# A fused convolution and token-mixing kernel: the transposes of u in the full final steps moved from TensorE to crossbar DMA transfers, and the channel mixes placed later

## The chip, the cores and the metric

The kernel runs on one NeuronCore of a Trainium2 chip. The rounds of runs fell on several chips; every ratio compares runs of the same rounds. Times are device microseconds of that core. Where a median is quoted, the number of runs stands beside it.

## The reference, cut to what matters

```python
# x: [8, 4224, 192] f32, a 7-tap softmax-weighted causal convolution comes first
x = lightweight_conv(x, weight)
theta = x @ w_theta
zr, zi = x * cos(theta), x * sin(theta)
y = einsum('ts,bsd->btd', w_tok_r, zr) + einsum('ts,bsd->btd', w_tok_i, zi)   # 4224 x 4224 each
u = x + y
out = u + maximum(u @ w_ch, 0)          # the channel mix
```

The last line is what the change is about. `u @ w_ch` contracts over the channels, and the kernel's matmul for it takes u with its channels on the partitions; the token mixing leaves u with tokens on the partitions. Every piece of u has to be transposed between the two.

## The kernel before

The token mixing runs in 58 steps. A step takes two blocks of 128 output rows and up to 11 chunks of 128 input tokens. A step with two blocks makes seven runs over the chunks (a seven-product scheme: two 2x2 block products in seven), each run two matmuls a chunk, y. (In this sense a run is a part of a step; elsewhere a run is an execution of a kernel.) After a run DVE adds the PSUM result into `pv` ("give"). DVE also prepares the weights of the next step: it turns four weight blocks (`turn`, a transpose on DVE) and makes four sums or differences of turned blocks (`wsum`, S1 to S4). The steps 41 to 57 are "final": they complete their rows, and the step after them casts u to f16 on ACT, transposes it on TensorE, copies it out of PSUM on ACT, mixes the channels (matmuls v) and stores. The steps 41 to 52 have all 11 chunks ("full final steps"); 53 to 57 have fewer and are called late.

```python
    def transposed(u, by_dve=False):
        tp = banks("tp", F16)
        for k in range(6):
            pe(nc.tensor.transpose(
                tp[:, 0, k * P : (k + 1) * P], u[:, k * P : (k + 1) * P], ident
            ))
        uT = wk.tile([P, 6, P], F16, name="uT", tag="uT")          # 2 buffers
        evacuate(uT[:, :, :].rearrange("p k s -> p (k s)"), tp[:, 0, 0 : 6 * P], by_dve)
        return uT
# [cut]
        def w_tasks(self):          # the weight blocks of the NEXT step, on DVE; time in units of runs
            return [
                (0.25, lambda: self.turn("11")), (1.2, lambda: self.turn("21")),
                (2.05, lambda: self.wsum("S3")), (2.2, lambda: self.turn("22")),
                (3.05, lambda: self.wsum("S1")), (3.3, lambda: self.wsum("S2")),
                (4.2, lambda: self.turn("12")), (5.1, lambda: self.wsum("S4")),
            ]
# [cut]
        def runs(self):             # weights, z, PSUM tile, opens it?, (row block, half, ...) of the sum
                return [
                    ("11", Z11, "c1", True, (0, 0, True)),
                    ("S1", T1, "c2", True, (1, 1, True)),
                    ("S2", T2, "c1", False, (0, 1, True)),
                    ("S4", Z22, "c2", False, (0, 1, False)),
                    ("S3", T3, "c1", False, (1, 1, False)),
                    ("12", Z21, "c3", True, (0, 0, False)),
                    ("22", T4, "c1", False, (1, 0, True)),
                ]
# [cut]
        def turn_u(self, i, g):
            self.uT[i, g] = transposed(self.ub[i, g])
# [cut]
        def outputs(self):
                # late steps: [cut]
                    at = 0.7 + 12 * i                      # us after the step's end, row block i
                    every, turn, mix = 3.6, 2.9, 4.7       # per column half g: cast, transpose, mix
                for g in range(NG):
                    found.append((at, lambda i=i, g=g: self.cast(i, g)))
                    found.append((at + turn, lambda i=i, g=g: self.turn_u(i, g)))
                    found.append((at + mix, lambda i=i, g=g: self.output(i, g)))
                    at += every
```

The PSUM tile c1 holds run 11, is then added to by run S2 (third) and by run S3 (fifth), and the sums are taken in between. So PE may not start run S3 before DVE has read c1 after run S2; this sum is called the third run's sum below. x is added to rows in two ways: for the steps 43 to 52 POOL adds a loaded tile (`xr`) to `pv` in SBUF, 3.1 us each, one step ahead, so during the steps 42 to 51; for the late steps an accumulating DMA, issued by POOL, adds x to the partial sums in DRAM, four steps ahead, so beside the steps 49 to 53. (For the steps 41 and 42 such transfers run ten steps ahead.)

## Time and profile before

| | before |
|---|---|
| median of 3 runs | 1468.77 us (1468.66 to 1469.96) |
| PE busy in the profiled run | 1434.6 us of 1469.8 |
| y matmul, start to start, in the final steps | 163 ns |
| v matmul, start to start | 82 ns |
| transpose, start to start | 56 ns |
| a full final step (steps 42 to 51) | 29.0 us |

The last four rows were worked out from the PE records of the trace: the median distance between starts, and the distance between the first y matmul of a step and that of the next. There are 7656 y matmuls in every kernel of this study, so steps can be laid side by side by counting them.

The page of the kernel before, its busy times and the chain that ended last:

```profile
PE 1434.6 (98%) x10095; PEld 905.6 (62%) x10095; DVE 1001.0 (68%) x1050; ACT 360.7 (25%) x461; POOL 430.3 (29%) x659
...
PE 91%; DVE 3%; ACT 3%; DMA 1%; issue 1%; POOL 0%; DVEq 0%; ACTq 0%; POOLq 0%
```

The table by stretches of the kernel before, for the steps 45, 51 and 52 (first column: from and to in us; the numbers follow the head line):

```profile
core 0: us, PE busy (x) PEld busy (x) DVE busy (x) ACT busy (x) POOL busy (x), PEclk, DMA share, GB/s
1137.40:1166.50 29.10, 29.10 (x213) 19.09 (x211) 22.20 (x19) 6.28 (x8) 10.83 (x10) 1.00 0.77 186
1311.90:1340.90 29.00, 29.00 (x212) 19.04 (x211) 25.61 (x19) 5.78 (x8) 15.53 (x16) 1.00 1.06 246
1340.90:1369.90 29.00, 29.00 (x212) 19.05 (x211) 18.25 (x19) 6.78 (x9) 8.19 (x12) 1.00 0.93 210
```

PE has no gap at all in these three steps: what is taken off it there should shorten the span. The DMA share is 0.77 in a middle step and about 1 in the last ones (it adds up packet times, so the 1.06 of step 51 means that packets of one engine overlapped).

Yet the trace held a warning: in step 48, where the sum ended at +16.62 us of the step in place of +16.09, PE did wait for it, 0.22 us just before run S3 (and in step 41 0.19 us). The author's list of waits from 1100 to 1380 us ends with step 48's:

```profile
PE y L408 <- DVE pv L373: 0.2, 1, 0.2
```

These are the 0.22 us that the prediction's 324.78 of 325 us lack.

### The profile page before, as it was taken

What the parts mean: (1) busy time and instruction counts of PE and PEld (TensorE: products, weight loads), DVE (VectorE), ACT (ScalarE), POOL (GpSimd) and SP (SyncE); (2) the same over time, 40 slices, a digit from 0 to 9 for tenths busy, and PEclk for the clock granted to TensorE, in tenths of its full rate; (3) what the DMA queues carried; (4) which work ended last, traced back from release to release, by engine and by line L of the source; (5) the groups of instructions that cost most, each with busy time, mean ns of one, the idle gap of its engine ahead of it and who ended that gap; (6) DMA issues with size and microseconds to landing.
All of it is one profiled execution on the core that took longest, in us unless ns stands there. A gap on an engine that the chain in (4) does not pass through costs nothing.

```text
span 1469.8 us, 24434 instructions
## 1 busy us (share of the span) xinstructions
PE 1434.6 (98%) x10095; PEld 905.6 (62%) x10095; DVE 1001.0 (68%) x1050; ACT 360.7 (25%) x461; POOL 430.3 (29%) x659
## 2 busy tenths in 40 slices
PE   7789999999999999999999999999999999999997
PEld 4556666666666666666666666666666666666665
DVE  6884655454548687766656658769777787778575
ACT  6861101111134353000000015254122222121224
POOL 7422211111223322211113232332233333453220
PEclk9999999999999999999999999999999999999998
DMA  9976756574699999887879989999778777999873
GB/s 172 227 155 145 144 104 144 96 151 89 149 232 212 232 224 263 193 198 167 209 162 239 200 194 229 201 232 256 128 191 197 173 182 185 224 237 217 196 201 108
DMA packets 234975, 274.16 MB, mean 187 GB/s; under 512 B 69104, under 2 KB 202608, under 8 KB 234864
## 3 DMA queue, kind: packets, MB, share of 16 engines
q0 software_dynamic: 163616, 95.30, 49.0%
q1 hardware_dynamic: 71248, 177.30, 34.1%
q8 instruction: 79, 1.29, 0.3%
q14 instruction: 32, 0.26, 0.1%
HBM read 245.49 MB, written 111.28 MB: 243 GB/s over the span
## 4 chain that ended last, share of the span: by engine, by line
PE 91%; DVE 3%; ACT 3%; DMA 1%; issue 1%; POOL 0%; DVEq 0%; ACTq 0%; POOLq 0%
PE y L408 81%; PE v L138 6%; PE tp L153 3%; ACT z L233 2%; PE pc L196 2%; DMA st<-in_moe_w_tok_i_dram 1%; DVE pv L373 1%; DVE z L244 1%; DVE z L238 0%; DVE wt L308 0%; DVE pv L437 0%; ACT uT L148 0%; DVE wt L320 0%; ACT pv L371 0%; ACT z L148 0%
## 5 line engine op out<-in xcount | busy, mean ns | idle before, releaser
L408 PE MATMUL y<-z,wt 128*128 128x384 f16 x7656 | 1295.3, 326 | 7.7 <-DVE pv L373 6.8
L408 PEld LDWEIGHTS <-wt 128*128 128x128 f16 x7656 | 737.5, 98 | 475.0 <-issue 10.4
L373 DVE TENSOR_TENSOR pv<-y,pv 128x768 f32<-128x768 f32 x324 | 308.5, 953 | 374.2 <-PE y L408 348.6
L308 DVE STREAM_TRANSPOSE wt<-st 128x1408 f16<-128x1408 f16 (+7 forms) x224 | 326.4, 1463 | 7.7 <-DMA st<-in_moe_w_tok_i_dram 7.0
L295 POOL DMA_DIRECT2D st<-in_moe_w_tok_i_dram x232 | 132.7, 581 | 497.7 <-DVE wt L308 473.7
L295 POOL DMA_DIRECT2D st<-in_moe_w_tok_r_dram x232 | 132.7, 581 | 459.0 <-DVE wt L308 443.7
L320 DVE TENSOR_TENSOR wt<-wt 128x1408 f16<-128x1408 f16 (+7 forms) x216 | 204.1, 945 | 9.5 <-PE y L408 6.6
L148 ACT ACTIVATE uT<-tp 128x768 f16<-128x768 f16 x127 | 102.3, 813 | 296.8 <-PE tp L153 294.9
L148 ACT ACTIVATE z<-pc 128x768 f16<-128x768 f32 x65 | 52.9, 814 | 386.5 <-PE pc L196 386.5
L371 ACT ACTIVATE pv<-y 128x768 f32<-128x768 f32 x66 | 53.7, 813 | 281.5 <-PE y L408 281.5
L138 PEld LDWEIGHTS <-uT 128*128 128x128 f16 x1056 | 93.0, 99 | 25.9 <-issue 9.9
L437 DVE SCALAR_TENSOR_TENSOR pv<-v,pv 128x768 f32<-128x768 f32 x66 | 62.7, 949 | 46.8 <-PE v L138 45.5
L183 POOL DMA_DIRECT2D xw<-in_x_dram x132 | 76.5, 591 | 35.8 <-issue 10.1
L427 ACT ACTIVATE ub<-pv 128x768 f16<-128x768 f32 x66 | 54.8, 837 | 90.6 <-DVE pv L373 89.5
L244 DVE TENSOR_TENSOR z<-z 128x768 f16<-128x768 f16 x132 | 73.4, 556 | 3.8
L233 ACT ACTIVATE z<-v,half_pi 128x768 f16<-128x768 f32 x66 | 59.6, 903 | 40.0 <-PE v L138 39.8
L238 DVE TENSOR_TENSOR z<-z 128x1536 f16<-128x1536 f16 x66 | 60.4, 950 | 10.8 <-ACT z L233 10.8
L355 POOL TENSOR_TENSOR pv<-pv,xr 128x1536 f32<-128x1536 f32 x20 | 62.9, 3144 | 7.9 <-issue 4.5
L138 PE MATMUL v<-wch,uT 128*128 128x192 f16 x528 | 56.9, 254 | 3.5 <-DVE pv L437 1.9
L138 PE MATMUL v<-wth,uT 128*128 128x192 f16 x528 | 54.3, 246 | 3.1 <-ACT z L233 3.0
L233 ACT ACTIVATE z<-v 128x768 f16<-128x768 f32 x66 | 53.2, 805 | 0.0
L153 PE MATMUL tp<-ident,z 128*128 128x128 f16 x396 | 33.4, 222 | 8.8 <-ACT z L233 8.3
(43 smaller groups left out, 201.5 us busy)
## 6 DMA issues: line engine op xcount, KB each, us to landing
part<-pv SPq DMA_DIRECT2D x79, 768.0 KB, 4.3
pv<-part SPq DMA_DIRECT2D x79, 768.0 KB, 5.4
out_dram<-pv SPq DMA_DIRECT2D x66, 384.0 KB, 4.5
st<-in_moe_w_tok_r_dram POOLq DMA_DIRECT2D x136, 176.0 KB, 5.8
st<-in_moe_w_tok_i_dram POOLq DMA_DIRECT2D x136, 176.0 KB, 4.9
xs<-z SPq DMA_DIRECT2D x132, 96.0 KB, 4.5
xw<-in_x_dram POOLq DMA_DIRECT2D x121, 96.0 KB, 5.9
part<-xs POOLq DMA_DIRECT2D x26, 384.0 KB, 7.4
```

The costliest lines, as they stand in the source:

```text
L138: pe(nc.tensor.matmul(v[:, k, b * D : (b + 1) * D], lhsT=tT[:, 3 * k + b + i, :], rhs=w[:, 2 * b + i, :], start=(i == 0), stop=(i == 1),))
L148: act(nc.scalar.activation(out=out, in_=in_, func=AT.Copy))
L153: pe(nc.tensor.transpose(tp[:, 0, k * P : (k + 1) * P], u[:, k * P : (k + 1) * P], ident))
L183: nc.gpsimd.dma_start(out=self.xw[lo : lo + n, h, :, :], in_=x[:, t0 : t0 + n, :].rearrange("b s d -> s b d"),)
L233: act(nc.scalar.activation(**args))
L244: dve(nc.vector.tensor_tensor(out=z[:, o, :], in0=z[:, a, :], in1=z[:, b, :], op=ALU.subtract))
L295: pool(nc.gpsimd.dma_start(out=st[a * Q : (a + 1) * Q, 0:nb, :, 0:n] .rearrange("i r bt s -> i (r bt) s"), in_=w[self.tbs[0] * P : (self.t ...
L308: dve(nc.vector.transpose(self.w[name][:, 0 : self.n, :, :], self.st[int(name[1])][:, int(name[0]) - 1, :, 0 : self.n * Q] .rearrange("p b ...
L320: dve(nc.vector.tensor_tensor(out=self.w[name][:, 0 : self.n, :, :], in0=self.w[a][:, 0 : self.n, :, :], in1=self.w[b][:, 0 : self.n, :, : ...
L355: pool(nc.gpsimd.tensor_tensor(out=self.pv[i], in0=self.pv[i], in1=xr, op=ALU.add))
L373: dve(nc.vector.tensor_tensor(out=o, in0=yv, in1=o, op=ALU.add))
L408: pe(nc.tensor.matmul(y[cn][:, q, 0:BH], lhsT=self.w[wn][:, c, :, :].rearrange("p bt i -> p (bt i)"), rhs=chunks[k].z[:, zn, q * BH : (q + ...
```

## The change

The intent: a DMA transpose (a crossing, below) takes u from SBUF to SBUF through the crossbar, so PE does 288 transposes less, ACT 48 copies out of PSUM less. As a DMA takes longer (the plain 384 KB stores landed in 4.5 us) than six transposes at 56 ns and a copy of 0.81 us, the mixes are placed 9 us behind the casts, casts start as early as the row block is complete, and uT has four buffers. Two buffers of uT cost more room than was free, so one of the eleven buffers of the turned weights (wt) is given up. Late steps stay on TensorE.

```diff
+    def turned():
+        return wk.tile([P, 6, P], F16, name="uT", tag="uT", bufs=4)
+
+    def crossed(u):
+        uT = turned()
+        nc.sync.dma_start(out=uT, in_=u, transpose=True)
+        return uT
# [cut]
-        uT = wk.tile([P, 6, P], F16, name="uT", tag="uT")
+        uT = turned()
# [cut]
-            return wpool.tile([P, NW, NQ, Q], F16, name="wt", tag="wt", bufs=11)
+            return wpool.tile([P, NW, NQ, Q], F16, name="wt", tag="wt", bufs=10)
# [cut]
-            self.uT[i, g] = transposed(self.ub[i, g])
+            self.uT[i, g] = (transposed if self.late else crossed)(self.ub[i, g])
# [cut]
-                    at = 0.7 + 12 * i
-                    every, turn, mix = 3.6, 2.9, 4.7
+                    at = (8.5 if i else 0.9 - self.time / 7) if self.pair else 0.7
+                    every, turn, mix = 3.6, 1.7, 9.0
```

## The prediction

> **What bounds the kernel now.** TensorE. The page gives PE 1434.6 us busy of 1469.8 (98%), and the chain that ended last is 91% PE. Where the change acts, the table by stretches has PE busy 324.78 us of the 325 us from 1050 to 1375 us, granted clock 1.00, DVE 76%, ACT 21%, POOL 39%, DMA share 0.60 to 1.07. Start to start there, a y matmul costs 163 ns, a v matmul 82 ns, a transpose 56 ns (medians of the PE records). The groups' 219 ns for a transpose is latency, not cost.
>
> **What the change removes.** The 12 final steps with all 11 chunks (two row blocks, two column halves each) lose 48 groups of six transposes: PE rows fall by 576, that is 288 matmuls with their weight loads. At 56 ns that is 288 x 0.056 = 16.1 us of PE, all on the chain because PE has no gap there. 48 copies of 0.81 us (39 us) leave ACT, which is idle four fifths of that stretch: worth nothing. Ceiling of the gain: 16 us, 1.1%, 1452.6 us.
>
> **What it adds.** 48 DMA transposes of 192 KB on SP's queue, and 2 more uT buffers, paid with one of 11 wt buffers. Latency: SP's plain 384 KB stores land in 4.5 us median, 768 KB loads in 5.4. The Trainium skill ("Advanced Engine Details and Errata", X-Bar Transpose) says that such transposes are as fast as regular DMAs; "VectorE: DVE Perf Modes", The three transpose paths, gives 1309 ns for 128x128 and 390 ns for TensorE. This trace's 56 ns cadence contradicts using the 390 as PE cost; no run yet shows the DMA figure. My estimate for 128x768 under this load: 4 to 7 us. DMA share should rise by 0.1 to 0.4 in these steps.
>
> **Room for the latency.** From the changed PE order: the last sum into row block 0 ends about 4 us before its step's end, cast done about 2 us later, transpose issued then; its mix stands 6.5 us into the next step. Room: 8 us for the first mix, 12 or more for the others. The tightest SP chain is stores, transposes, then the second xr load and POOL's 3.1 us add: done about 7 to 9 us into the step, needed by a sum at 7.8 us, which PE needs only at 12.1 us. Each wt buffer still comes free 23 us before its next contents are first used. So I expect no new PE wait of note, 1 to 4 us in total.
>
> **Prediction.** 1455.5 us (13 us gained); 8 in 10 between 1450 and 1472. Faster by over 2%: 0.01; within 2%: 0.91; slower by over 2%: 0.08.
>
> **What would show it.** PE records: no transposes from ub before the late steps; y to y still 163 ns; PE busy still about 25 of 25 us per stretch; a full final step about 1.3 us shorter; ACT busy down by 39 us; the v matmuls waiting for no DMA.
>
> **What would make it wrong.** The transposes take over 8 us, or occupy the 16 DMA engines much longer than a copy of the same bytes: then PE waits at the first mix of each of 12 steps (each us over is about 12 us of time), or st loads land late and DVE's turns hold up PE. Or the transposes keep SP busy for several us each, so that xr and pv loads come late.

## More of the kernel before

DVE is busy three quarters of the time. That looks like room. It is not, as the timeline of step 45 shows (start, duration, engine, line, operation; a count x42 merges matmuls that follow one another):

```profile
1145.86 0.96 DVE L373 TENSOR_TENSOR pv<-y,pv 128x768 f32<-128x768 f32 x1 [0.66 <-PE y L408]
...
1146.40 3.12 POOL L355 TENSOR_TENSOR pv<-pv,xr 128x1536 f32<-128x1536 f32 x1
...
1146.73 3.55 DVE L320 TENSOR_TENSOR wt<-wt 128x1408 f16<-128x1408 f16 x1
...
1148.54 6.99 PE L408 MATMUL y<-z,wt 128*128 128x384 f16 x42
1150.20 1.63 DVE L308 STREAM_TRANSPOSE wt<-st 128x1408 f16<-128x1408 f16 x1
1151.76 0.91 DVE L437 SCALAR_TENSOR_TENSOR pv<-v,pv 128x768 f32<-128x768 f32 x1
1152.61 0.93 DVE L373 TENSOR_TENSOR pv<-y,pv 128x768 f32<-128x768 f32 x1
```

DVE works without a break from the second run's sum (1145.86) to the third run's sum, which ends at 1153.54. The first matmul of run S3 lies inside the x42 group, at 1153.74: the sum is ready 0.2 us before PE needs it. Nothing waits in this step, so no view of waits shows it.

## The result and the profile after

| | before | after |
|---|---|---|
| median of 4 runs each | 1469.05 us | 1464.09 us (1463.01 to 1467.40) |
| ratio | | 0.9969, 95% interval 0.9952 to 0.9986 |
| PE busy, profiled run | 1434.6 us | 1418.8 us |
| span, profiled run | 1469.8 us | 1463.0 us |

Ratios in this document are the mean time of one kernel's fast runs over that of the other's fast runs of the same rounds, so not quite the ratio of the medians quoted. The gain is 5 us where 13 was forecast. A later set of 6 runs gave 1466.32 us (1463.54 to 1470.34), ratio 0.9975.

The page of the changed kernel, the same two lines:

```profile
PE 1418.8 (97%) x9807; PEld 886.8 (61%) x9807; DVE 992.6 (68%) x1050; ACT 324.2 (22%) x413; POOL 429.2 (29%) x659
...
PE 80%; DVE 8%; DMA 5%; ACT 3%; issue 2%; POOL 0%; SPq 0%; DVEq 0%; ACTq 0%; POOLq 0%
```

PE lost 15.8 us of work, as forecast. But the chain that ended last now runs 80% over PE in place of 91%, with 8% over DVE and 5% over DMA: PE waits for others. The list of waits of the whole changed kernel has, for DVE's sums (6.8 us in the kernel before) and for the crossings:

```profile
PE y L417 <- DVE pv L382: 10.0, 15, 1.8
...
PE v L138 <- DMA uT<-ub: 6.2, 5, 2.1
```

The table by stretches of the changed kernel, for the steps 44, 51 and 52:

```profile
1107.90:1136.10 28.20, 27.85 (x189) 17.71 (x187) 22.09 (x19) 3.26 (x4) 10.82 (x10) 1.00 1.04 218
1305.50:1333.90 28.40, 27.86 (x188) 17.55 (x186) 19.80 (x19) 3.26 (x4) 14.27 (x14) 1.00 1.14 237
1333.90:1367.30 33.40, 28.20 (x188) 17.46 (x186) 18.15 (x19) 3.26 (x4) 12.92 (x15) 1.00 1.18 234
```

PE is no longer busy for the whole of a step: 27.85 of 28.20 us in a middle one, 28.20 of 33.40 in step 52. Laid side by side by y matmuls, the two profiled runs differ like this:

| part of the run | before | after | gained | possible by the transposes alone |
|---|---|---|---|---|
| up to step 41 | 1024.09 | 1025.56 | -1.47 | 0 |
| step 41 | 26.34 | 26.07 | +0.28 | 0 |
| steps 42 to 51 | 290.43 | 282.30 | +8.13 | 13.4 (10 x 24 x 0.056) |
| step 52 | 29.00 | 33.38 | -4.38 | 1.3 |
| steps 53 to 56 | 77.68 | 77.05 | +0.6 | 1.3 |
| step 57 and the end | 22.2 | 18.6 | +3.6 | 0 |
| sum | 1469.8 | 1463.0 | +6.8 | 16.1 |

(The sum is above 5 us because the profiled run of the kernel before took 1471.56 us.) So there are three things to explain: 5.3 us that the steps 42 to 51 did not give, about 6 us lost in the steps 52 and 53 (5.7 and 0.7), and 3.6 us that came from the end of the program, where nothing was transposed by DMA.

The timeline of step 44 of the changed kernel, for the first:

```profile
1115.35 0.96 DVE L446 SCALAR_TENSOR_TENSOR pv<-v,pv 128x768 f32<-128x768 f32 x1 [1.09 <-PE v L138]
...
1116.22 0.95 DVE L382 TENSOR_TENSOR pv<-y,pv 128x768 f32<-128x768 f32 x1
...
1116.87 3.11 POOL L364 TENSOR_TENSOR pv<-pv,xr 128x1536 f32<-128x1536 f32 x1
1117.09 3.65 DVE L329 TENSOR_TENSOR wt<-wt 128x1408 f16<-128x1408 f16 x1
...
1119.31 4.39 PE L417 MATMUL y<-z,wt 128*128 128x384 f16 x26
1120.66 1.63 DVE L317 STREAM_TRANSPOSE wt<-st 128x1408 f16<-128x1408 f16 x1
1122.22 0.91 DVE L446 SCALAR_TENSOR_TENSOR pv<-v,pv 128x768 f32<-128x768 f32 x1
1123.07 0.93 DVE L382 TENSOR_TENSOR pv<-y,pv 128x768 f32<-128x768 f32 x1
...
1124.05 3.73 PE L417 MATMUL y<-z,wt 128*128 128x384 f16 x22 [0.35 <-DVE pv L382]
```

The third run's sum ends at 1124.00 and PE's run S3 starts at 1124.05, after a wait. In step 45 of each kernel, counted from the step's first y matmul, this sum ends at +16.09 us before and at +16.09 us after. DVE's chain did not become shorter; PE's part of the step did, and would have been there at +15.62. The profile's 0.35 us is less than the whole loss: from one y matmul to the next it is 0.67 to 0.68 us here in place of 0.163, so 0.52 us a step in the steps 43 to 47. The ten steps are not alike: 42 loses 0.44 us, 48 and 49 lose 1.05 and 0.87, all before run S3; step 50 loses nothing, since there POOL's add came later and the subtraction (L329) took 0.88 us; and the 0.7 us of step 51 are a wait for a crossing. So of the 5.3 us about 4.6 are DVE's chain (5.0 less the 0.4 that step 48 lost before) and 0.7 DMA.

For the second, the timeline of the changed kernel around step 52 (SPq is SP's queue; L451 stores, L363 loads xr, L353 loads pv, L156 is the crossing, L138 the mix):

```profile
1318.52 2.21 SPq L451 DMA_DIRECT2D out_dram<-pv  x2
1320.82 5.10 SPq L363 DMA_DIRECT2D xr<-xs  x1
...
1335.13 0.34 SPq L353 DMA_DIRECT2D pv<-part  x1
...
1336.37 1.51 SPq L156 DMA_TRANSPOSE uT<-ub  x1
...
1338.61 3.14 SPq L156 DMA_TRANSPOSE uT<-ub  x1
...
1342.65 0.83 PE L138 MATMUL v<-wch,uT 128*128 128x192 f16 x8 [2.06 <-DMA uT<-ub]
...
1348.17 0.83 PE L138 MATMUL v<-wch,uT 128*128 128x192 f16 x8 [1.10 <-DMA uT<-ub]
...
1358.84 0.83 PE L138 MATMUL v<-wch,uT 128*128 128x192 f16 x8 [2.04 <-DMA uT<-ub]
```

Three of the four mixes of this step wait for a crossing. The first crossing is issued 2.4 us after the step's start (1333.93), where in step 44 it was issued 2.0 us before it: SP stood at the pv load (L353), which waited for the two stores of 1318.52, landed 13.9 and 15.9 us after their issue. The crossings also take longer to land. From issue to landing they took, in the stretch up to 1270 us and in the one after it (minimum, median, maximum):

```profile
DMA to landing us min/median/max: 2.5/5.3/7.7
...
DMA to landing us min/median/max: 5.5/9.6/15.3
```

The second stretch is where the accumulating transfers for the late steps run. They did so before as well, but no mix depended on a DMA then.

### The profile page after: what moved, and what is told of

The parts are those of the page before. It is cut to its first block, busy times and chain, and to the rows that moved or that the text cites. A ratio compares the mean times of both kernels' runs of the same rounds, so it can differ in the third digit from the quotient of the medians.

```text
span 1463.0 us, 23889 instructions
## 1 busy us (share of the span) xinstructions
PE 1418.8 (97%) x9807; PEld 886.8 (61%) x9807; DVE 992.6 (68%) x1050; ACT 324.2 (22%) x413; POOL 429.2 (29%) x659
## 4 chain that ended last, share of the span: by engine, by line
PE 80%; DVE 8%; DMA 5%; ACT 3%; issue 2%; POOL 0%; SPq 0%; DVEq 0%; ACTq 0%; POOLq 0%
PE y L417 72%; PE v L138 5%; DVE pv L382 2%; ACT z L242 2%; DVE wt L317 2%; DVE wt L329 2%; DMA out_dram<-pv 1%; PE pc L205 1%; PE tp L162 1%; DVE pv L446 1%; DMA uT<-ub 1%; DVE z L253 1%; DMA xw<-in_x_dram 1%; DVE z L247 1%; DMA st<-in_moe_w_tok_r_dram 1%
## 5 line engine op out<-in xcount | busy, mean ns | idle before, releaser
L317 DVE STREAM_TRANSPOSE wt<-st 128x1408 f16<-128x1408 f16 (+7 forms) x224 | 326.4, 1462 | 26.6 <-PE y L417 19.7
L329 DVE TENSOR_TENSOR wt<-wt 128x1408 f16<-128x1408 f16 (+7 forms) x216 | 196.1, 908 | 21.8 <-PE y L417 18.2
L138 PEld LDWEIGHTS <-uT 128*128 128x128 f16 x1056 | 91.0, 98 | 32.3 <-issue 8.8
L148 ACT ACTIVATE uT<-tp 128x768 f16<-128x768 f16 x79 | 63.3, 813 | 65.9 <-PE tp L162 65.9
L364 POOL TENSOR_TENSOR pv<-pv,xr 128x1536 f32<-128x1536 f32 x20 | 62.8, 3138 | 30.6 <-DMA xr<-xs 22.2
L247 DVE TENSOR_TENSOR z<-z 128x1536 f16<-128x1536 f16 x66 | 60.3, 949 | 11.7 <-ACT z L242 11.7
L138 PE MATMUL v<-wch,uT 128*128 128x192 f16 x528 | 54.3, 246 | 8.6 <-DMA uT<-ub 6.2
L138 PE MATMUL v<-wth,uT 128*128 128x192 f16 x528 | 55.0, 248 | 3.1 <-ACT z L242 3.0
```

What stands on the lines that cost most here:

```text
L138: pe(nc.tensor.matmul(v[:, k, b * D : (b + 1) * D], lhsT=tT[:, 3 * k + b + i, :], rhs=w[:, 2 * b + i, :], start=(i == 0), stop=(i == 1),))
L148: act(nc.scalar.activation(out=out, in_=in_, func=AT.Copy))
L247: dve(nc.vector.tensor_tensor(out=o, in0=xv, in1=o, op=ALU.mult))
L317: dve(nc.vector.transpose(self.w[name][:, 0 : self.n, :, :], self.st[int(name[1])][:, int(name[0]) - 1, :, 0 : self.n * Q] .rearrange("p b ...
L329: dve(nc.vector.tensor_tensor(out=self.w[name][:, 0 : self.n, :, :], in0=self.w[a][:, 0 : self.n, :, :], in1=self.w[b][:, 0 : self.n, :, : ...
```

## The experiments

Twelve runs (e11 is the changed kernel again, e12 is e5 again). Theory, formed from the two traces: (A) the 0.5 us a step is DVE's chain to the third run's sum, and DMA has no part in it; (B) the loss in the last full steps is crossings that come late where the accumulating transfers share the DMA engines with them; (C) the 3.6 us at the end come of the four uT buffers, and the 1.5 us at the start are variation. Rivals: DMA contention causes A as well; SP's order causes B; the lost wt buffer costs something.

### e1_bufs: the buffer counts alone

```diff
 # on the kernel before
-            return wpool.tile(... name="wt", tag="wt", bufs=11)
+            return wpool.tile(... name="wt", tag="wt", bufs=10)
-        uT = wk.tile([P, 6, P], F16, name="uT", tag="uT")
+        uT = wk.tile([P, 6, P], F16, name="uT", tag="uT", bufs=4)
```

> The kernel before with only the buffer counts of the change (4 uT buffers, 10 wt buffers), TensorE transposes kept. My theory: the 1.5 us that the changed kernel lay behind before its final steps, and the 3.6 us that it gained in the last 20 us, are not of the crossbar: the first is run-to-run variation, the second comes of the uT buffers. Then all full final steps stay at 29.0 us, the stretch before them is within 1 us of before, the tail is 1 to 4 us shorter, total 1465 to 1469 us. Rival: the eleventh wt buffer was worth something: DVE waits for wt buffers lengthen steps before the final ones, total 1470 us or more.

Measured: 1468.00 us median of 4 runs against 1470.92 of 7, ratio 0.9984 (0.9967 to 1.0). Up to step 41 it lies 0.1 us behind the kernel before, all full final steps take 29.0 us (step 49: 29.2), and step 57 with the end takes 18.5 us in place of 22.2. So the lost wt buffer costs nothing that shows, and the end is 3.6 us shorter by the uT buffers; e3_extra, with ten wt buffers but two of uT, still has 22.2 there. How they shorten it was not traced. The lag at the start is variation of step 0: it took 19.6 us in some profiled runs (before, e1, e10, e12) and 20.3 to 21.0 in others (after, e2, e3, e4, e11); both occur with ten wt buffers.

### e2_noturn: no transposes at all

```diff
 # on the changed kernel
-        uT = turned()
-        nc.sync.dma_start(out=uT, in_=u, transpose=True)
-        return uT
+        return nothing          # one tile of zeros, written once
```

> The changed kernel with no transposes at all: the channel mixes read one fixed tile of zeros (wrong result on purpose), casts and order kept. My theory: the 0.5 us that PE waits in each of the steps 42 to 51 is for DVE's sum of the third run and has nothing to do with DMA, so those steps stay at 28.1 to 28.2 us; only the loss in step 52 (33.4 us) goes, to about 28.2; total about 1458 us (1456 to 1460). Rival (DMA contention causes both losses): the steps fall to 27.66 us and the total to about 1453.

Measured: 1457.78 us (4 runs), wrong result as intended. Steps 43 to 47 take 28.18 to 28.20 us, so PE's wait is there without a single crossing; step 45 again has the sum end at +16.10 us and PE wait for it:

```profile
1144.01 3.67 DVE L329 TENSOR_TENSOR wt<-wt 128x1408 f16<-128x1408 f16 x1
...
1150.01 0.94 DVE L382 TENSOR_TENSOR pv<-y,pv 128x768 f32<-128x768 f32 x1
...
1150.99 1.30 PE L417 MATMUL y<-z,wt 128*128 128x384 f16 x7 [0.37 <-DVE pv L382]
```

Steps 52 and 53 take 27.66 and 22.79 us: the loss there is gone. The first rival falls: the 0.5 us is not of DMA.

### e3_extra: the crossings alone, PE's transposes kept

```diff
 # on the kernel before, 10 wt buffers
         def turn_u(self, i, g):
+            if not self.late:
+                spare_uT = wk.tile([P, 6, P], F16, name="spare_uT", tag="spare_uT", bufs=2)
+                nc.sync.dma_start(out=spare_uT, in_=self.ub[i, g], transpose=True)
             self.uT[i, g] = transposed(self.ub[i, g])
```

> The kernel before, TensorE transposes kept, with 48 crossbar transposes added whose result nobody reads (10 wt buffers for the room): the DMA load alone. My theory: DMA share rises by about 0.25 in the full final steps, PE does not wait for it, steps stay at 29.0 us, total 1467 to 1471 us. Rival (the added DMA load delays loads and sums): steps 42 to 51 lengthen by 0.3 us or more, the steps 50 to 52 by some us, total above 1473.

Measured: 1487.75 us (4 runs), ratio 1.0121. The steps 42 to 51 stay as they were (29.0 us, step 48 29.4 as before), but step 52 takes 30.8 us and step 53 36.2 in place of 24.1. The forecast of the total was wrong: I had not thought of the cast buffers. The unread crossings hold `ub` (two buffers) until they land, 5.4 to 17.9 us after issue in this stretch, ACT's casts wait 40.6 us for that between 1270 and 1430 us, and PE waits for the casts. The run says two things: in the steps 42 to 51 the added crossings cost PE nothing, and in the last full steps they are late for whoever needs them, also when PE needs their result not at all.

### e4_give: one DVE instruction moved

```diff
 # on the changed kernel, w_tasks
-                (2.05, lambda: self.wsum("S3")), (2.2, lambda: self.turn("22")),
+                (2.05, lambda: self.wsum("S3")),
+                (3.0 if self.final else 2.2, lambda: self.turn("22")),
```

> The changed kernel with one DVE instruction moved: the turn of weight block 22 of the next step stands behind the sum of the third run instead of ahead of it, in final steps. My theory: that sum ends 1.6 us earlier, PE's wait at the start of run S3 (0.5 us a step) goes, steps 42 to 51 fall from 28.2 to 27.7 us, total about 1459 us (1457 to 1461); step 52 stays long. Rival: the wait is caused by late DMA or moves to another run at once: steps stay at 28.1 to 28.2, total 1463 to 1466.

Measured: 1464.43 us, with a wide spread (1459.91, 1461.37, 1467.48, 1471.31). The timeline of its step 45:

```profile
1143.10 3.66 DVE L329 TENSOR_TENSOR wt<-wt 128x1408 f16<-128x1408 f16 x1
...
1145.32 5.36 PE L418 MATMUL y<-z,wt 128*128 128x384 f16 x32
1146.68 0.94 DVE L447 SCALAR_TENSOR_TENSOR pv<-v,pv 128x768 f32<-128x768 f32 x1
1147.54 0.94 DVE L383 TENSOR_TENSOR pv<-y,pv 128x768 f32<-128x768 f32 x1
1148.41 1.63 DVE L317 STREAM_TRANSPOSE wt<-st 128x1408 f16<-128x1408 f16 x1
```

The turn (L317) now stands behind the sum (L383), which ends at +14.56 us of the step; PE starts run S3 at +15.62 without a wait. Steps 42 to 49 take 27.66 us each, exactly 29.00 less 24 x 0.056. Theory A holds. But in the profiled run (1467.48 us) the steps 50, 51 and 52 now take 30.8, 34.1 and 33.7 us: 15.7 us more than three steps of 27.66. The total did not move because what A gave, B took. That B grew was not forecast; the same transfers have less time per step then, but that this is the reason is only argued.

### e5_first8 and e12_first8: crossings only in the steps 41 to 48

```diff
 # on e4_give
+            self.crosses = self.final and self.t < 49
-            ... (transposed if self.late else crossed)(...)
+            ... (crossed if self.crosses else transposed)(...)
 # steps 49 to 52 also get the old places: at = 0.7 + 12 * i; every, turn, mix = 3.6, 2.9, 4.7
```

> e4_give with the crossbar kept only for the first 8 of the 12 full final steps (41 to 48); the steps 49 to 52 transpose on TensorE at the old places. My theory: the crossings are late only where the accumulating transfers for the short last steps (from about 1261 us on) share the DMA engines with them; so the loss of 16 us in steps 50 to 52 goes, and with it 5.4 us of the gain. Steps 42 to 48 at 27.7 us, steps 50 to 52 at 29.0, total 1455 to 1458 us, with a spread of the runs below 3 us. Rival (late crossings come of too little room for any crossing): PE waits stay in some steps, total above 1460.

Measured: 1456.70 us (4 runs, 1456.46 to 1458.63), ratio 0.9907. Steps 42 to 49 take 27.66 us, 50 to 52 take 29.0, no PE wait over 0.3 us stands between step 42 and step 52. As forecast.

> e5_first8 once more, beside the changed kernel on the same chip: 1455 to 1459 us, 0.4 to 0.7% faster than the changed kernel, spread of the fast runs below 3 us.

Repeated beside the changed kernel: 1457.06 us (1456.26 to 1458.98), ratio to before 0.9911 (0.9899 to 0.9924). The changed kernel on the same chip:

> The changed kernel itself once more, for a comparison on the same chip and to see whether its losses repeat: steps 43 to 47 at 28.2 us, step 52 longer than 30 us, total 1463 to 1468 us.

1466.32 us, ratio 0.9975 (0.9960 to 0.9989). Its profiled run has steps 43 to 47 at 28.17 to 28.19 us, step 52 at 33.34, and this time step 53 at 27.3 in place of 24.1. Both losses repeat. The kernel with eight crossed steps is 0.64% faster than the changed one (0.9911 / 0.9975), and beats both kernels of the case.

### e6_actq: crossings from ACT's queue

```diff
 # on e4_give
-        nc.sync.dma_start(out=uT, in_=u, transpose=True)
+        act(nc.scalar.dma_start(out=uT, in_=u, transpose=True))
```

> e4_give with all crossings issued from ACT's queue in place of SP's, nothing else. Theory 1 (SP's own order is the cause: a crossing stands behind stores and loads of pv that wait for landings, and its issue of 1.2 to 6 us holds up what follows): the crossings of the steps 49 to 52 are issued within 3 us of their casts, PE's waits in steps 50 to 52 fall from 16 to under 5 us, total 1449 to 1454 us. Theory 2 (the DMA engines are overloaded there): crossings still take 9 to 16 us to land, waits stay above 8 us, total 1456 to 1466.

Measured: 1468.15 us, ratio 0.9977. The crossings are now issued on time (step 52: 2.1 us before the step's start), but take longer: the first crossing of a step landed in 8.1 to 9.4 us for the steps 44 to 48 (median 8.2) where e4_give shows 5.5 to 7.7 (median 6.6). PE waits in most steps from 45 on, and steps 50, 52 and 53 still lose 4.1, 2.6 and 5.1 us. Theory 1 falls as a remedy: freeing the crossings from SP's order does not help. The total is even above the range given for theory 2. Why crossings on a queue of their own land later is left open; that they then run beside the stores and loads, no longer between them, is a guess.

### e7_adds: the accumulating transfers ten steps ahead

```diff
 # on e4_give
-            if s.ahead and t == s.t - (4 if s.late else 10):
+            if s.ahead and t == s.t - 10:
```

> e4_give with the accumulating transfers of the late steps issued 10 steps ahead in place of 4, so beside steps 43 to 47. Theory 2 (load): steps 50 to 52 fall from 31 to 34 us to below 28.5, some waits appear in steps 43 to 47, where DMA share rises above 1.1; total 1449 to 1460. Theory 1 (SP's order): the waits in 50 to 52 stay above 8 us in sum, total 1458 to 1466.

Measured: 1476.83 us, ratio 1.0046. The table by stretches of its steps 44, 45 and 50:

```profile
1106.10:1138.40 32.30, 29.66 (x188) 18.30 (x186) 19.84 (x19) 3.37 (x4) 14.26 (x14) 0.95 1.08 231
1138.40:1172.60 34.20, 29.70 (x188) 18.14 (x186) 19.75 (x19) 3.26 (x4) 14.26 (x14) 0.95 1.04 227
1302.70:1330.30 27.60, 27.60 (x187) 17.66 (x186) 19.66 (x19) 3.26 (x4) 11.28 (x10) 1.00 1.09 234
```

The loss went where the transfers went: steps 44 to 48 take 32.3 to 35.3 us, steps 49 to 52 take 27.66. Theory 2 was right in kind and its forecast of the size wrong: with five steps hit in place of three, the total is worse than before, and the DMA share of those steps is not above 1.1. The first two lines also show why some waits cost more than themselves: the granted clock of the stretch falls to 0.95. After four of the six waits of 2.7 to 4.3 us (not after one of 2.8 in step 46 and one of 3.4 in step 47) the y matmuls follow at 320 ns for some 2 to 3 us, in place of 163. And the DMA share does not tell the bad steps from the good ones: 1.04 to 1.08 against 1.09.

### e9_actadds: both

```diff
 # e6_actq and e7_adds together
```

> e6_actq and e7_adds together. If order and load each hold a part: the lowest total of the four, 1447 to 1452 us, with all full final steps at 27.7 to 28.2 us. If the load alone decides: within 2 us of e7_adds. If the order alone decides: within 2 us of e6_actq.

Measured: 1469.50 us, ratio 0.9996. The total fits the third outcome, 1.35 us over e6_actq in the median; the steps do not: 44 to 48 take 29.4 to 33.3 us and 49 to 52 take 27.66, where e6_actq lost its time in 50, 52 and 53 too. So the total alone would have misled. The loss again sits where the accumulating transfers are, with the crossings on either queue.

### e10_noadds: no accumulating transfers for the late steps

```diff
 # on e4_give
-            if s.ahead and t == s.t - (4 if s.late else 10):
+            if s.ahead and not s.late and t == s.t - 10:
```

> e4_give without the accumulating transfers of the late steps (their rows miss x: wrong result on purpose), crossings in all 12 full final steps. My theory, that these transfers on top of the crossings make the crossings of steps 49 to 52 late: all steps 42 to 52 at 27.7 us, total 1449 to 1453 us. Rival (the stretch from 1270 us on is short of DMA or SP time also without them): waits of 5 us and more stay in steps 50 to 52, total above 1455.

Measured: 1453.69 us (4 runs, 1452.16 to 1453.76), wrong result as intended. The table by stretches of its steps 44 and 52:

```profile
1106.40:1134.10 27.70, 27.70 (x188) 17.73 (x187) 22.23 (x19) 3.26 (x4) 10.83 (x10) 1.00 1.13 219
...
1327.70:1355.40 27.70, 27.70 (x189) 17.73 (x187) 18.06 (x19) 3.26 (x4) 4.58 (x8) 1.00 1.14 196
```

All eleven steps 42 to 52 take 27.66 us, with all twelve crossed; the median is just above the range given. Theory B holds: without these transfers there is no loss, and where they go it goes. Still, the crossings of this kernel took 6.6 to 11.7 us to land from 1270 to 1345 us. What differs from the changed kernel, beside the longest landings (15.3 us there), is that the first crossing of step 52 was issued on time, 2 us before the step's start: the two stores that SP's pv load ahead of it waited for landed in 8.4 and 8.2 us here, 13.9 and 15.9 there. So the accumulating transfers act in two ways, by longer landings and through SP's order, and e6_actq shows that the second alone is not the whole. POOL issues these transfers and is busy with each for 0.8 to 1.7 us in the changed kernel; no run separates that from their load on the DMA engines.

### e13_s3late: the DVE order mended another way

```diff
 # on e5_first8
-                (2.05, lambda: self.wsum("S3")),
-                (3.0 if self.final else 2.2, lambda: self.turn("22")),
+                (3.02 if self.final else 2.05, lambda: self.wsum("S3")),
+                (2.2, lambda: self.turn("22")),
```

> e5_first8 with the DVE order mended another way: the turn of block 22 stays where the change had it, and the subtraction that makes S3 stands behind the sum of the third run, after POOL's 3.1 us add has ended. My theory: it is this subtraction, held up by the add (3.65 us in place of 0.9), that pushes the sum past the moment PE needs it; moved, it takes 0.9 us, DVE's busy time falls by about 2.7 us in each of these steps, PE's wait at run S3 is gone as in e5_first8: steps 42 to 49 at 27.7 us, total 1455 to 1459. Rival (the order alone counts, the add does not lengthen it): it takes 3 us or more at the new place too and steps stay above 28.

Measured: 1457.25 us (1457.19 to 1457.60), ratio 0.9911. The timeline of its step 45:

```profile
1142.77 3.12 POOL L366 TENSOR_TENSOR pv<-pv,xr 128x1536 f32<-128x1536 f32 x1
1142.99 1.64 DVE L318 STREAM_TRANSPOSE wt<-st 128x1408 f16<-128x1408 f16 x1
...
1145.49 0.96 DVE L448 SCALAR_TENSOR_TENSOR pv<-v,pv 128x768 f32<-128x768 f32 x1 [0.86 <-PE v L138]
1146.37 0.95 DVE L384 TENSOR_TENSOR pv<-y,pv 128x768 f32<-128x768 f32 x1
1147.23 2.61 DVE L330 TENSOR_TENSOR wt<-wt 128x1408 f16<-128x1408 f16 x3
```

Beside POOL's add the turn takes its usual 1.64 us. The subtraction that makes S3 is now the first of the three merged in the last line, which take 0.87 us each; where it met the add it took 3.65. DVE's busy time from 1080 to 1246 us, six steps, falls from 133.9 us (e5_first8) to 117.4, 2.7 us a step. The steps take 27.66 us, so PE loses nothing, and the total equals that of e5_first8. The Trainium skill ("SBUF — State Buffer", Who interferes with whom) states that a DVE instruction with two SBUF inputs contends with a GpSimd instruction that reads SBUF, for a pair of ports held as an exclusive lock. The traces agree: in step 44 of the changed kernel POOL's add starts first, the subtraction starts 0.2 us later and ends 0.76 us after it. The section also says that the order of issue decides who blocks; the recorded starts do not settle that: in step 48 of the kernel before, the subtraction starts 0.20 us ahead of the add, takes 4.08 us and again ends 0.76 us after it.

### All runs

| kernel | median us (runs) | ratio to before | steps 42 to 49 | steps 50, 51, 52 |
|---|---|---|---|---|
| after | 1464.09 (4) | 0.9969 | 28.1 to 28.7 | 27.7, 28.4, 33.4 |
| e11_after | 1466.32 (6) | 0.9975 | 28.1 to 28.7 | 28.3, 28.7, 33.3 |
| e1_bufs | 1468.00 (4) | 0.9984 | 29.0 to 29.4 | 29.0, 29.0, 29.0 |
| e2_noturn (wrong) | 1457.78 (4) | 0.9913 | 28.1 to 28.7 | 28.2, 28.2, 27.7 |
| e3_extra | 1487.75 (4) | 1.0121 | 29.0 to 29.4 | 29.0, 29.0, 30.8 |
| e4_give | 1464.43 (4) | 0.9963 | 27.66 | 30.8, 34.1, 33.7 |
| e5_first8 | 1456.70 (4) | 0.9907 | 27.66 | 29.0, 29.0, 29.0 |
| e12_first8 | 1457.06 (4) | 0.9911 | 27.66 | 29.0, 29.0, 29.0 |
| e6_actq | 1468.15 (4) | 0.9977 | 27.7 to 29.4 | 31.8, 27.7, 30.3 |
| e7_adds | 1476.83 (4) | 1.0046 | 27.7 to 35.3 | 27.66 each |
| e9_actadds | 1469.50 (4) | 0.9996 | 27.7 to 33.3 | 27.66 each |
| e10_noadds (wrong) | 1453.69 (4) | 0.9884 | 27.66 | 27.66 each |
| e13_s3late | 1457.25 (4) | 0.9911 | 27.66 | 29.0, 29.0, 29.0 |

Steps are those of one profiled run per kernel.

## Why the prediction was right or wrong

- Right: PE bounds these steps, and the transposes cost it 56 ns each, 16.1 us in all. e10_noadds shows each step shorter by 1.34 us, which is 24 x 0.056. ACT's busy time fell by 36.5 us and the DMA share of a middle step rose from 0.77 to 1.04, within the 0.1 to 0.4 given.
- Right for the steps up to 1270 us: the crossing's latency. The estimate was 4 to 7 us, the median 5.3 (2.5 to 7.7), and no mix waited for one there.
- Wrong, the step that failed first: "So I expect no new PE wait of note, 1 to 4 us in total." It had two holes.
  - The room was worked out for the crossings, for SP's chain and for the wt buffers, but not for the DVE instruction that PE itself waits for in every step. Of the sums in its chain, only the one that needs xr was looked at. The third run's sum had 0.2 us to spare in the kernel before, PE became 0.67 us earlier at that point, and 0.52 us were lost in a middle step: most of the 5.3 us over the steps 42 to 51 (0.7 us in step 51 was a crossing). e2_noturn shows that the wait needs no crossing; e4_give and e13_s3late show that a change of DVE's order alone takes it away. One such wait of 0.2 us already stood in the list of waits of the kernel before.
  - One latency was used for all twelve steps. The DMA share that the prediction itself quoted runs from 0.60 to 1.07, and its high end lies in the steps where the accumulating transfers run. There the crossings took 9.6 us in the median and up to 15.3, and SP issued them up to 4.5 us later than elsewhere. About 6 us were lost in the steps 52 and 53; e10_noadds, without the accumulating transfers, loses nothing there. The prediction named both paths among what would make it wrong, and gave them too little weight.
- Not foreseen, so luck: four uT buffers shorten the end of the program by 3.6 us, as e1_bufs shows. The prediction counted the buffers only as a cost. Without this the change would have gained only 1 to 3 us (5 us by the medians or 6.8 by the profiled runs, less 3.6).
- In sum: that PE bounds the steps and what the transposes cost it was right; the term that was mis-sized is the new PE waits, 1 to 4 us forecast, about 12 measured (5.3 in the steps 42 to 51, 5.7 in step 52, 0.7 in step 53), and DVE's sum, most of the 5.3, was named among what would make it wrong only by way of late loads. The 3.6 us at the end stand against them.

## What to carry to other kernels

Where PE is busy without a gap, taking work from it moves the limit to whatever was ready just in time: before trusting the saving, list for every PE wait in the program (not only the new one) how long its input was ready ahead, above all the PSUM reads by DVE that leave no idle time and so appear in a list of waits late or not at all; a wait of 0.2 us in one of ten like steps deserves a look. A latency hidden behind compute must be checked also in the stretch where other large transfers run, and on a queue that issues in order, an entry that waits for a landing should not stand ahead of a transfer that PE needs (SP's pv load in step 52). Here the steps that used the transfers gave their gain whole once these were only those of the stretch without the extra load and one DVE instruction was moved: 1457 us in place of 1464 to 1466.

## What the Trainium skill lacked or had wrong

- "Advanced Engine Details and Errata", X-Bar Transpose (TRN2), says that transposing DMAs are as fast as regular ones. Between 1100 and 1370 us the crossings' 256 B packets took 18 ns in the median and 31 in the mean. Plain packets on the same queue took 36 and 41 at 768 B, 121 and 142 at 3072 B; drawn on in a line to 256 B, that is an estimate of 17 and 19. So the medians agree and the mean is longer; why is not shown. What the section lacks is the spread: nearly alone a crossing of 192 KB landed in 2.5 us, beside the accumulating transfers in up to 15.3, where plain stores too took up to 15.9.
- The issue of such a transfer from SP took 1.2 to 4.1 us in the changed kernel (median 1.25), where a plain pv load took 0.34 in the median. "DMA: Bandwidth & Descriptors", DMA Transpose (X-bar), gives no issue time; the page's sequencer times for a DMA transpose are for trn3 and "previous generations", none for this chip by name. It matters on an in-order queue.
- "VectorE: DVE Perf Modes", The three transpose paths, compares TensorE at 390 ns with the crossbar at 1309 ns for 128x128. In a stream of matmuls TensorE's transpose cost 56 ns of PE time here; the table would need a column for throughput.
- "SBUF — State Buffer", Who interferes with whom, agrees with the runs on the contention (3.65 us in place of 0.9 for the blocked subtraction); its rule that the order of issue decides could not be read off the recorded starts (4.08 us for a subtraction that started first).
- "DMA: Bandwidth & Descriptors", Issuing engines are not separate DMA queues, says that issuing from several engines saves only the sequencer's time. It says nothing of what moving a transfer to another queue does to its landing: from ACT's queue (e6_actq) the first crossing of a step landed in 8.2 us in the median, from SP's (e4_give) in 6.6.
